# Feed-forward matmuls as pairs on 64 rows that swap PSUM banks halfway, in an attention kernel on one core

## The chip, the core and the metric

The kernel runs on one core of a Trainium2 chip. The core has five engines, each with its own in-order queue of instructions: TensorE (PE) multiplies matrices into PSUM, VectorE (DVE), ScalarE (ACT) and GpSimd (POOL) work element by element, and SyncE (SP) mostly issues transfers between HBM and the on-chip memory. Engines wait for each other through semaphores. PSUM has eight banks of 128 partitions x 512 floats. The metric is the device time of one execution in microseconds (us); smaller is better.

## The reference

With x of 2048 rows and 512 columns, the output is a gated mix of an attention and a feed-forward block:

```python
g = _sigmoid((x * gate_w).sum(-1, keepdims=True))
q = (x @ wq).reshape(B, S, H, Dh)            # 32 heads of 16, S = 2048
k = x @ wk; v = x @ wv                       # one key and value head for all
p = _softmax(einsum("bhqd,bkd->bhqk", q, k) * Dh ** -0.5)
a = (p @ v, heads side by side) @ wo
b = (_gelu(x @ w_gate) * (x @ w_up)) @ w_down     # 512 -> 1376 -> 512
return g * a + (1 - g) * b
```

All data are float32. Each of the 32 heads has 2048 x 2048 scores, and every one of them goes through an exponential.

## The kernel before

The rows of x are cut into four groups of 512 (tg). A prologue projects q, k and v. To keep nearly float32 precision with matmuls that take a rounded operand, each operand is split into a high and a low part (hh and hl, gh and gl, woh and wol), and a product is the sum of three matmuls: high x high, high x low, low x high. The prologue ends with a branch on a flag that all engines read (line 445); its true side is not taken here.

The main loop has 32 units u (a row group, and four heads), each with 16 key chunks kc of 128 keys. A *score step* (`scores`, line 488) fills one of three two-bank PSUM buffers with two matmuls on 51 rows each, one on partitions 0 to 50 and one on 64 to 114, and ACT exponentiates the 128 x 1024 scores into one of twelve buffers p. Two score steps feed one *value step* (`pv`, line 564): four matmuls, each on its own 32 output partitions, that add into the accumulator `acc` in a bank of its own. The chip runs each of these four as two records. After 16 value steps `norm` (line 506) reads the accumulator. For the first unit of a pair it writes two masked copies; for the second it adds to them and queues the division in small parts in the list `bg`, which `slot` hands out one by one after every third feed-forward matmul.

The feed-forward work is the filler between the attention steps. The 1376 hidden columns are cut into 11 chunks of 128, for each of the four row groups: 44 chunks. A chunk's gate output g and up output u take 12 matmuls each (four slices of x, three products); three chunks (at a row group's end two) then give four down outputs of nine (or six) matmuls. When the attention of a row group is done, four outputs of 12 matmuls multiply it by wo. Each output is one call of the generator `units` (line 405): all its matmuls in a row, on 128 rows, into the one bank `pf`, and then a DVE operation that reads it. DVE makes the high parts of the weights (line 105) and POOL the low parts (line 106).

The order is written out by hand: the instructions are recorded as they stand. `ORDER` (line 42) is a unit's pattern, in which S is a score step, V3 three value steps and F one whole feed-forward output:

```python
ORDER = ("V3 SSS F SSS V2 SS V2 SSS F SSS V3 SSS F SSS V3 SSS F SSS V3 SSS F SSS").split()
```

`defer(k, fn)` puts off work by k score steps; `run_later` issues it. SP issues nearly all transfers, in its order: weights (line 205), q (lines 244 and 245), x and wo (line 224), outputs (line 326). PSUM is full: three score buffers of two banks, the accumulator, and `pf`.

Of the kernel before, what the change touches and what calls it, by code (L numbers as in the profile page):

```python
# [19 lines left out]
P = 128  # L20
# [21 lines left out]
ORDER = ("V3 SSS F SSS V2 SS V2 SSS F SSS V3 SSS F SSS V3 SSS F SSS V3 SSS F SSS").split()  # L42
# [3 lines left out]
def mix_kernel(ctx, tc, xT, wq, wkv, wo, wf, out):  # L46
# [3 lines left out]
    ps_s = ctx.enter_context(tc.tile_pool(name="ps_s", bufs=3, space=PSUM))  # L50
    ps_a = ctx.enter_context(tc.tile_pool(name="ps_a", bufs=1, space=PSUM))
    ps_f = ctx.enter_context(tc.tile_pool(name="ps_f", bufs=1, space=PSUM))
    ctx.enter_context(tc.manual_schedule())

# [152 lines left out]
    def split_w(n, lo=None):  # L207
        if n not in stage:
            return
# [5 lines left out]
        lo = lo or nc.gpsimd  # L215
        for t in range(2):
            split(nc.vector, lo, gh[:, t], gl[:, t], st[:, t].rearrange("p (c f) -> p c f", c=NC))
        split(nc.vector, lo, dh, dl, st[:, 2])
        W[n] = gh, gl, dh, dl

    def fetch_split(name, src, hi, lo, h=0):
        cs = slice(2 * h, 2 * h + 2)
        t = cp.tile([P, 2, D], F32, tag="xst", name=f"{name}{h}", bufs=1)
        nc.sync.dma_start(t, src[:, cs])

        def go():
            split(nc.vector, nc.gpsimd, hi[:, cs], lo[:, cs], t)
            if h == 0:
                fetch_split(name, src, hi, lo, 1)

        defer(6, go)

    def reload_x(tg):
        xs[tg] = x_tiles(tg)
        fetch_split(f"xst{tg}_", xT[tg], *xs[tg])
# [3 lines left out]
    def load_qk(t, u):  # L239
        g, ub = divmod(u, 8)  # L240
        b, a = divmod(ub, 2)
        for j in range(2):
            hs = slice(4 * a + j, 4 * a + 4, 2)
            nc.sync.dma_start(t[64 * j : 64 * j + 32].bitcast(F32), scr[g, b, 0:32, hs])
            nc.sync.dma_start(t[64 * j + 32 : 64 * j + KR].bitcast(F32), scr[g, b, 0:16, hs])

    def load_q(u, shift=True, data=True):
        g, ub = divmod(u, 8)
        if data:
            Q[u] = cp.tile([P, 2, TG], F32R, tag="Q", name=f"Q{u}", bufs=2)  # L250
            load_qk(Q[u], u)
        if shift:
            for j in range(2):
                nc.sync.dma_start(Q[u][64 * j + KR : 64 * j + QK].bitcast(F32), shs[g, :, 4 * ub + j : 4 * ub + 4 : 2])
# [3 lines left out]
    for ti, tg in enumerate(order):  # L258
# [4 lines left out]
        for b in range(NB):  # L263
            pq = ps_s.tile([P, 2 * TG], F32, tag="s", name=f"pq{tg}_{b}")[:, 0:TG]
# [5 lines left out]
            if ti == NTG - 1 and b == 0:  # L270
                split_w(0)
            if ti == NTG - 1 and b == 1:
                post_v()
            if ti == NTG - 1 and b == 2:
                load_q(0)
                load_q(1)

    def pairmax():
        pm = ps_s.tile([P, 2 * TG], F32, tag="s", name="pm")[0:1, 0 : 2 * P]
# [12 lines left out]
    peak = []  # L292
    O = {}
    bg = []

    def slot():
        if bg:
            bg.pop(0)()

    def flush():  # L300
        while bg:
            slot()

    wo_jobs = []
    done = [0]

    def pass_list(n):
        return [(i, a, b) for i in range(n) for a, b in ((0, 0), (0, 1), (1, 0))]

    def chain_mm(ps, terms, first=True, last=True):  # L310
        for q, (a, b) in enumerate(terms):
            nc.tensor.matmul(ps, a, b, start=(first and q == 0), stop=(last and q == len(terms) - 1),  # L312
                             skip_group_check=True)
            if q % EVERY == EVERY - 1:
                slot()
            if q == 8 and not peak:
                peak.append(pairmax())
# [10 lines left out]
    def wo_job(g):  # L328
        for i in range(4):
            ps = ps_f.tile([P, D], F32, tag="pf", name=f"wo{g}_{i}")  # L330
            chain_mm(ps, [t for bl in range(NB) for t in wo_terms(g, i, bl)])
            wo_out(g, i, ps)
            yield

    def run_jobs():
        while wo_jobs and wo_jobs[0][0] <= now[0]:
            yield from wo_job(wo_jobs.pop(0)[1])

    def down(batch):
        tg, f = chunks[batch[0][0]]  # L340
        if f == 0:
            acc[tg] = mp.tile([P, 4, D], F32, tag="acc", name=f"acc{tg}", bufs=2)
        for i in range(4):
            ps = ps_f.tile([P, D], F32, tag="pf", name=f"dn{batch[0][0]}_{i}")
            ts = slice(i * P, (i + 1) * P)
            chain_mm(ps, [(a[:, ts], b) for n, hh, hl in batch for dh, dl in (W[n][2:],)
                          for a, b in ((hh, dh), (hh, dl), (hl, dh))])
            o = acc[tg][:, i]
            w = gc[:, 4 * tg + i : 4 * tg + i + 1]
            if f == 0:  # L350
                nc.vector.tensor_scalar(o, ps, w, None, op0=ALU.mult)
            else:
                nc.vector.scalar_tensor_tensor(o, ps, w, o, op0=ALU.mult, op1=ALU.add)  # L353
            yield

    def project(n, t, ps):
        gh, gl = W[n][:2]
        xh, xl = xs[chunks[n][0]]
        chain_mm(ps, [(w[:, t, c], x[:, c]) for c in range(NC) for w, x in ((gh, xh), (gh, xl), (gl, xh))])

    def gate_up(n, hold):
        split_w(n)
        ps = ps_f.tile([P, TG], F32, tag="pf", name=f"g{n}")
        project(n, 0, ps)
        gs = cp.tile([P, TG], F32, tag="gs", name=f"gs{n}", bufs=1)
        sq = cp.tile([P, TG], F32, tag="sq", name=f"sq{n}", bufs=1)
        nc.vector.tensor_copy(gs, ps)  # L367

        def inner():
            nc.vector.scalar_tensor_tensor(sq, gs, GC, gs, op0=ALU.mult, op1=ALU.mult)  # L370
            nc.vector.scalar_tensor_tensor(sq, sq, 1.0, gs, op0=ALU.add, op1=ALU.mult)

        def tanh():
            nc.scalar.activation(sq, sq, AF.Tanh, bias=0.0, scale=GS)  # L374

        def outer():
            nc.vector.scalar_tensor_tensor(sq, sq, 1.0, gs, op0=ALU.add, op1=ALU.mult)  # L377

        chain = [inner, tanh, outer]

        def advance():
            if chain:
                chain.pop(0)()

        for k in (1, 4, 6):
            defer(k, advance)
        yield
        if n == 0:
            ps = ps_a.tile([P, TG], F32, tag="pa", name="u0")
        else:  # L390
            ps = ps_f.tile([P, TG], F32, tag="pf", name=f"u{n}")
        project(n, 1, ps)
        if n == 0:
            yield
        while chain:
            advance()
        hh = cp.tile([P, TG], F32R, tag="hh", name=f"hh{n}", bufs=3)
        hl = cp.tile([P, TG], F32R, tag="hl", name=f"hl{n}", bufs=3)
        nc.vector.scalar_tensor_tensor(gs, ps, 0.5, sq, op0=ALU.mult, op1=ALU.mult)  # L399
        nc.vector.tensor_copy(hh, gs)  # L400
        nc.vector.tensor_sub(hl, gs, hh)
        hold.append((n, hh, hl))
        yield

    def units():
        hold = []
        for n, (tg, f) in enumerate(chunks):
            if n > 0:
                fetch_w(n + 1)
            if n > 0:  # L410
                defer(2 if n == 1 else 8, lambda n=n: split_w(n + 1))
            if n == 2:
                fetch_split("wo", wo, woh, wol)
            yield from gate_up(n, hold)
            if f == NF - 1 and tg + 1 < NTG:
                reload_x(tg + 1)
            if f % 3 == 2 or f == NF - 1:
                yield from down([hold.pop(0) for _ in range(len(hold))])
            yield from run_jobs()

    filler = units()
    nsteps = 8 * NTG * NKC

    def fill(k=1):
        for _ in range(k):
            next(filler, None)
# [7 lines left out]
    fill()  # L434
    fill()
# [3 lines left out]
    split_w(1)  # L439
# [5 lines left out]
    with tc.If(v > 0):  # L445
        with tc.tile_pool(name="gp", bufs=1) as gp:
# [4 lines left out]
            for g in range(NTG):  # L451
                mx = gp.tile([P, 4, H, 2], F32, tag="mx", name=f"mx{g}")
                for ub in range(8):
                    t = gp.tile([P, 2, TG], F32R, tag="gq", name=f"gq{g}_{ub}", bufs=2)
                    load_qk(t, 8 * g + ub)
                    for i in range(4):
                        for h in range(4):
                            rs = slice(64 * (h % 2), 64 * (h % 2) + KR)
                            for e in range(2):
                                ps = ps_s.tile([P, 2 * TG], F32, tag="s", name="gs")  # L460
# [27 lines left out]
    def scores(n):  # L488
        s, pr = divmod(n, 2)
        if s >= nsteps:  # L490
            return
# [5 lines left out]
        ps = ps_s.tile([P, 2 * TG], F32, tag="s", name="s")  # L497
# [8 lines left out]
    def norm(u):  # L506
        g, ub = divmod(u, 8)
        b, a = divmod(ub, 2)
        ac = accp.pop(u)
        if a == 0:  # L510
            flush()
            t = mp.tile([P, TG], F32, tag="nt", name=f"nt{u}", bufs=1)
            tz = mp.tile([P, TG], F32, tag="ntz", name=f"ntz{u}", bufs=1)
# [4 lines left out]
        t, tz = at.pop((g, b))  # L518
        N, z = t, tz
        r = mp.tile([P, TG], F32, tag="nr", name=f"nr{u}", bufs=1)  # L520
# [128 lines left out]
```

## Time and profile before

| | us |
|---|---|
| median of 3 runs | 1304.97 (1304.6 to 1305.59) |
| the profiled execution | 1304.42 |
| its span, first to last instruction | 1302.6 |
| PE busy in it | 1284.3 (99%) |
| ACT busy | 1023.1 (79%) |
| DVE busy | 554.3 (43%) |
| POOL busy | 213.2 (16%) |

Times are counted from the start of the span. In a timeline each row has its start, its length, the engine, the line of the kernel, the operation, the output and its inputs, and how many records were merged; a bracket names idle time ahead of it and what ended it. PE's matmul records overlap, as the next one starts before the last has drained: what one costs is read from start to start. In the rows of groups the first two numbers behind the bar are the busy time in us and the mean of one in ns; the third is the idle time of the engine just before them. PEld is the load of a matmul's weights, which can run under the matmul before. In a table by stretches the columns are the length, and each engine's busy time with its number of records (PE, PEld, DVE, ACT, POOL), then the granted PE clock, the share of the DMA engines and GB/s.

### The profile page before, as it was taken

The page shows a single profiled execution, that of the slowest core. Times are in us where ns is not written, and L with a number is a line of the kernel's source. Part 1 is how long each engine was busy: PE and PEld are TensorE (multiplying, and loading weights), DVE is VectorE, ACT ScalarE, POOL GpSimd, SP SyncE. Part 2 cuts the span into 40 slices and gives each one's busy share as a digit, 9 for nine tenths or more (in the row PEclk, how much of TensorE's full clock was granted, in tenths as well). Part 3 has the DMA queues.
Part 4 walks back from the last instruction along what each step waited for, and adds up shares of the span by engine and source line. Part 5 has one row for each costly group of instructions (what it writes and reads, how often), then busy time and mean ns, then how long its engine had stood idle before and what let it go on. Part 6 is the DMA issues. An engine that isn't in the chain of part 4 may idle for free.

```text
span 1302.6 us, 20297 instructions
## 1 busy us (share of the span) xinstructions
PE 1284.3 (99%) x8180; PEld 647.7 (50%) x8180; DVE 554.3 (43%) x821; ACT 1023.1 (79%) x1118; POOL 213.2 (16%) x172
## 2 busy tenths in 40 slices
PE   9979999999999999999999999999999999999998
PEld 6845445444444444444444554444544454454444
DVE  6763442616352162633426144352526143434344
ACT  5348888888888788888888878878887788888883
POOL 3132121203021021210312011021122011202110
PEclk9989999999999999999999999999999999999999
DMA  8432101111110111111200021110121211001100
GB/s 310 182 102 78 38 15 48 38 62 39 69 38 14 58 61 38 62 37 54 68 19 30 22 86 38 62 38 14 50 70 38 70 38 62 19 20 62 38 1 33
DMA packets 25205, 72.43 MB, mean 56 GB/s; under 512 B 3889, under 2 KB 3921, under 8 KB 25105
## 3 DMA queue, kind: packets, MB, share of 16 engines
q1 hardware_dynamic: 24704, 70.02, 16.0%
q8 instruction: 66, 1.08, 0.3%
q0 software_dynamic: 256, 0.79, 0.1%
q10 hardware_dynamic: 144, 0.26, 0.1%
q14 instruction: 35, 0.28, 0.1%
HBM read 57.67 MB, written 13.37 MB: 55 GB/s over the span
## 4 chain that ended last, share of the span: by engine, by line
PE 82%; DVE 7%; ACT 3%; issue 1%; POOL 0%; DVEq 0%; ACTq 0%
PE acc L570 33%; PE s L500 21%; PE dn L312 9%; PE g L312 8%; PE u L312 8%; ACT p L503 3%; PE wo L312 3%; DVE ntz L536 2%; DVE oh L542 1%; DVE dh L105 1%; DVE nt L539 0%; DVE nr L527 0%; DVE ntz L530 0%; DVE ol L545 0%; DVE nt L533 0%
## 5 line engine op out<-in xcount | busy, mean ns | idle before, releaser
L503 ACT ACTIVATE p<-s 128x1024 f32<-128x1024 f32 x1024 | 972.2, 1027 | 224.9 <-PE s L500 224.5
L570 PE MATMUL acc<-p,v 128*32 128x512 f32 x4096 | 479.2, 597 | 0.0
L500 PE MATMUL s<-Q,kp 51*128 51x512 f32 x2048 | 338.9, 430 | 11.7 <-SPq L445 6.4
L500 PEld LDWEIGHTS s<-Q,kp 51*128 51x128 f32 x2048 | 165.5, 185 | 251.9 <-issue 169.8
L106 POOL TENSOR_TENSOR gl<-st,gh 128x512 fp32r<-128x512 f32 x88 | 122.3, 1409 | 1001.5 <-DVE gh L105 780.9
L570 PEld LDWEIGHTS acc<-p,v 128*32 128x32 f32 x4096 | 113.5, 109 | 259.7 <-issue 252.6
L353 DVE SCALAR_TENSOR_TENSOR acc<-dn,gc,acc 128x512 f32<-128x512 f32 x48 | 35.6, 742 | 206.8 <-PE dn L312 206.8
L367 DVE COPY gs<-g 128x512 f32<-128x512 f32 x44 | 30.4, 691 | 176.3 <-PE g L312 176.2
L312 PE MATMUL dn<-dh,hh 128*128 128x512 f32 x176 | 76.0, 432 | 0.0
L312 PE MATMUL g<-xh,gh 128*128 128x512 f32 x176 | 74.4, 423 | 0.0
L312 PE MATMUL u<-xh,gh 128*128 128x512 f32 x176 | 73.7, 419 | 0.6 <-DVE gs L367 0.6
L312 PE MATMUL g<-xh,gl 128*128 128x512 f32 x176 | 70.0, 398 | 0.3 <-POOL gl L106 0.3
L312 PE MATMUL g<-xl,gh 128*128 128x512 f32 x176 | 69.6, 395 | 0.0
L312 PE MATMUL dn<-dl,hh 128*128 128x512 f32 x176 | 69.0, 392 | 0.0
L312 PE MATMUL u<-xl,gh 128*128 128x512 f32 x176 | 68.8, 391 | 0.0
L312 PE MATMUL dn<-dh,hl 128*128 128x512 f32 x176 | 68.8, 391 | 0.0
L312 PE MATMUL u<-xh,gl 128*128 128x512 f32 x176 | 68.7, 390 | 0.0
L399 DVE SCALAR_TENSOR_TENSOR gs<-u,sq 128x512 f32<-128x512 f32 x44 | 29.9, 679 | 86.5 <-PE u L312 86.3
L105 DVE CAST dh<-st 128x512 fp32r<-128x512 f32 x44 | 64.2, 1459 | 0.0
L106 POOL TENSOR_TENSOR dl<-st,dh 128x512 fp32r<-128x512 f32 x44 | 61.7, 1403 | 0.0
L536 DVE RECIPROCAL ntz<-nr 128x128 f32<-128x128 f32 (+1 forms) x62 | 56.3, 949 | 0.6
L377 DVE SCALAR_TENSOR_TENSOR sq<-sq,gs 128x512 f32<-128x512 f32 x44 | 32.7, 743 | 55.3 <-ACT sq L374 55.3
(113 smaller groups left out, 974.6 us busy)
## 6 DMA issues: line engine op xcount, KB each, us to landing
st<-wf SPq DMA_DIRECT2D x44, 768.0 KB
scr<-q SPq DMA_DIRECT2D x16, 512.0 KB
Q<-scr SPq DMA_DIRECT2D x64, 128.0 KB
Q<-scr SPq DMA_DIRECT2D x64, 64.0 KB
out<-acc SPq DMA_DIRECT2D x16, 256.0 KB
xr<-xT SPq DMA_DIRECT2D x6, 512.0 KB
xst<-xT SPq DMA_DIRECT2D x6, 512.0 KB
xr<-xT SPq DMA_DIRECT2D x4, 256.0 KB
```

Source lines behind the costliest of these rows:

```text
L105: eng_h.tensor_copy(hi, src)
L106: eng_l.tensor_sub(lo, src, hi)
L312: nc.tensor.matmul(ps, a, b, start=(first and q == 0), stop=(last and q == len(terms) - 1), skip_group_check=True)
L353: nc.vector.scalar_tensor_tensor(o, ps, w, o, op0=ALU.mult, op1=ALU.add)
L367: nc.vector.tensor_copy(gs, ps)
L377: nc.vector.scalar_tensor_tensor(sq, sq, 1.0, gs, op0=ALU.add, op1=ALU.mult)
L399: nc.vector.scalar_tensor_tensor(gs, ps, 0.5, sq, op0=ALU.mult, op1=ALU.mult)
L500: nc.tensor.matmul(ps[:, j * TG : (j + 1) * TG], kp[rs, kc * P : (kc + 1) * P], Q[u][rs, pr], start=True, stop=True)
L503: nc.scalar.activation(p, ps, AF.Exp, bias=0.0, scale=SCALE)
L536: nc.vector.reciprocal(z[:, cs], r[:, cs])
L542: nc.vector.tensor_copy(oh[:, cs], N[:, cs])
L570: nc.tensor.matmul(accp[u][32 * j : 32 * j + 32], vt[:, kc], pb[s, j // 2][:, (j % 2) * TG : (j % 2 + 1) * TG], start=(kc == 0), stop=(kc ...
```

## The change

Two feed-forward outputs, z and y, are now computed together as a *job*: gate and up of one chunk, or two of four down outputs, or two of four wo outputs. Every matmul is cut into two of 64 rows. In a first pass over all terms z takes the lower 64 rows of the operands and y the upper 64, pair by pair; in a second pass they swap. Each output adds up in its own bank: y in `pf`, z in one half of the third score buffer, which is lent to the job (the word H) and given back at its end (R). In the meantime score steps use the two other buffers. [...]

Job orders are written out in `WORDS`. In them S is a score step, F3 three pairs and V2 a visit of about two value steps, which is cut where a unit ends or scores are not yet there (`visit` carries the rest over). G and L are gate jobs, D and E the two jobs of a batch of three chunks, d and e those of two, W a wo job, T the rest. The tanh chain of a gate job is put off by 3, 5 and 6 score steps. Splits of weights, x and wo are handed out between pairs like the parts of `norm`; x and wo come in quarters, and weights are fetched two chunks ahead. `norm` now copies the accumulator at once and works from the copy. In the prologue the first two loads of q and the shift rows of kp go through ACT's queue.

```diff
-ORDER = ("V3 SSS F SSS V2 SS V2 SSS F SSS V3 SSS F SSS V3 SSS F SSS V3 SSS F SSS").split()
+WORDS = {
+    "L": "S2 H F3 S F3 S F6 S2 F6 S F6 R S",
+    "G": "V2 S2 V H V F S2 F6 S F3 S F2 S F3 S F3 S F6 R S2 V2 S3 V",
+    "W": "V2 S2 H V2 S F S F6 S F2 S V S F3 S V S F S F S F2 S F3 S V S F6 S R S2",
+    "D": "V H V S2 V2 S2 F6 S F3 S V S F S F5 S F3 S R",
+    "E": "V S3 H V3 S F3 S F6 S2 F6 S F3 R S V2 S3",
+    "d": "V S V H S F3 S F3 S V S F2 S F4 R",
+    "e": "V S V S V S H F3 S F3 S V2 S F5 S F R S",
+    "T": "V2 S3",
+}
...
+    def two_banks(name):
+        i = next(i for i in turn if i not in held)
+        turn.remove(i)
+        turn.append(i)
+        return ps_s.tile([P, 2 * TG], F32, tag=f"s{i}", name=name)
...
+            if ti == NTG - 1 and b >= 2:
+                load_q(b - 2, q=nc.scalar)
...
-            nc.sync.dma_start(kp[r : r + 1].bitcast(F32), row.bitcast(F32))
+            nc.scalar.dma_start(kp[r : r + 1].bitcast(F32), row.bitcast(F32))
...
+    def pair_mm(z, y, X, Y):
+        for half in range(2):
+            for q in range(len(X)):
+                for j, (ps, (a, b)) in enumerate(((z, X[q]), (y, Y[q]))):
+                    lower = (j + half) % 2
+                    rs = slice(64 * lower, 64 * lower + 64)
+                    mm = nc.tensor.matmul(ps, a[rs], b[rs], start=(half == 0 and q == 0),
+                                          stop=(half == 1 and q == len(X) - 1), skip_group_check=True)
+                    if half == 1 and q == 0:
+                        after(mm.ins, relay[0])
...
+                if half == 0 and q == len(X) - 1:
+                    relay = nc.gpsimd.memset(mark, 0.0).ins
+                    for name in behind:
+                        after(relay, name)
+                    relay = [relay.name]
+                if q % EVERY == EVERY - 1 and (half == 0 or q + 4 <= len(X)):
+                    slot(half == 1 or q + 6 <= len(X))
+                yield
...
+    def gate_job(n):
+        tg, f = chunks[n]
+
+        def begin():
+            flush(todo)
+            if n == 1:
+                fetch_w(2)
+            fetch_w(n + 2)
...
+            defer(5 if n == 1 else 2, lambda: todo.extend(split_w(n + 1)))
+            return weights_terms(n, 0), weights_terms(n, 1)
+
+        def end(z, y):
+            gelu(n, z, lambda: y)
+            advance(3)()
+            for k, m in ((3, 2), (5, 1), (6, 0)):
+                defer(k, advance(m))
...
-            nc.vector.tensor_scalar(t, ac, mk, None, op0=ALU.mult)
-            nc.vector.tensor_scalar(tz, ac, mkb, None, op0=ALU.mult)
-            at[g, b] = t, tz
+            nc.vector.tensor_copy(c0, ac)
+            bg.append(lambda: nc.vector.tensor_scalar(t, c0, mk, None, op0=ALU.mult))
+            bg.append(lambda: nc.vector.tensor_scalar(tz, c0, mkb, None, op0=ALU.mult))
+            at[g, b] = c0, t, tz
...
+        c1 = ac
+        if not last:
+            c1 = new("n1")
+            nc.vector.tensor_copy(c1, ac)
...
+    def visit(k):
...
+        want = k + carry[0]
+        left = NKC - at_v[0] % NKC
+        ready = at_s[0] // 2 - at_v[0]
+        take = max(min(want, left, ready, 4), 0)
+        if left - take == 1 and take < 3 and ready > take:
+            take += 1
+        carry[0] = want - take
...
+            elif t[0] == "H":
+                advance(1)()
+                held.add(2)
+                z = ps_s.tile([P, 2 * TG], F32, tag="s2", name="z")[:, 0:TG]
+                y = ps_f.tile([P, TG], F32, tag="pf", name="y")
+                pairs = pair_mm(z, y, X, Y)
+            elif t[0] == "F":
+                for _ in range(k):
+                    next(pairs)
+            else:
+                assert next(pairs, None) is None
+                held.discard(2)
+                turn.remove(2)
+                turn.append(2)
+                job[2](z, y)
```

More of the change, by code (lines that the diff above doesn't have):

```diff
@@ L313, in chain_mm, with after @@
                              skip_group_check=True)
[L314 to L317, printed above, removed]
+    mark = cp.tile([1, 1], F32, name="mark")
+    SYNC = mybir.DependencyInfo(mybir.DependencyClass.Sync, mybir.DependencyReason.DATA)
+    def after(ins, name):
+        tc.add_manual_dep(ins, name, SYNC, reason="a bank passes from one row tile to the other")
+    def pair_mm(z, y, X, Y):
[8 more added lines that the diff above has]
+                        after(mm.ins, relay[0])
+                    if half == 0 and q == 0 and j == 0:
+                        behind = [None, None]
+                    behind[j] = mm.ins.name
+                if half == 0 and q == len(X) - 1:
[6 more added lines that the diff above has]
+                yield
@@ L326, in wo_out @@
         nc.sync.dma_start(out[g * TG + i * P : g * TG + (i + 1) * P], o)
[L328 to L403, printed above, removed]
@@ new lines, in score @@
+    def score():
+        scores(at_s[0])
+        at_s[0] = min(at_s[0] + 1, 2 * nsteps)
+    def visit(k):
+        if at_v[0] == nsteps:
+            return
+        flush(chain if at_v[0] == 0 else [])
+        want = k + carry[0]
[5 more added lines that the diff above has]
+        carry[0] = want - take
+        for _ in range(take):
+            pv(at_v[0])
+            at_v[0] += 1
+        if take and at_v[0] % NKC == 0:
+            if at_v[0] == nsteps:
+                ends.append(None)
+            else:
+                norm(at_v[0] // NKC - 1)
@@ L598, in mix_kernel @@
+    ends = []
+    chain.pop(0)()
+    for k, m in ((2, 2), (4, 0)):
+        defer(k, advance(m))
+    for job in jobs():
+        play(WORDS[job[0]], job)
+    while at_v[0] < nsteps:
+        play(WORDS["T"])
+    flush(chain)
+    flush(todo)
+    now[0] += 16
+    run_later()
+    norm(8 * NTG - 1)
     g = NTG - 1
-    tail = [ps_s.tile([P, 2 * TG], F32, tag="s", name=f"wos{h}")[:, 0:TG] for h in range(3)]
+    tail = [two_banks(f"wos{h}")[:, 0:TG] for h in range(3)]
     tail.append(ps_f.tile([P, TG], F32, tag="pf", name="wof"))
```

259 lines of the change are left out of this document (159 added, 100 removed), and 1 row of the table WORDS.

## The prediction

> **What bounds the kernel now.** I read the page's busy shares first, then its chain that ended last, then who TensorE (PE) waited for.
>
> ```profile
> span 1302.6 us, 20297 instructions
> PE 1284.3 (99%) x8180; PEld 647.7 (50%) x8180; DVE 554.3 (43%) x821; ACT 1023.1 (79%) x1118; POOL 213.2 (16%) x172
> PE 82%; DVE 7%; ACT 3%; issue 1%; POOL 0%; DVEq 0%; ACTq 0%
> L503 ACT ACTIVATE p<-s 128x1024 f32<-128x1024 f32 x1024 | 972.2, 1027 | 224.9 <-PE s L500 224.5
> ```
> ```profile
> PE s L500 <- SPq L445: 6.4, 1, 6.4
> PE s L500 <- ACT p L503: 5.3, 20, 0.3
> ```
> ```profile
> 74.50:1286.00 1211.50, 1205.32 (x7843) 586.11 (x7844) 490.81 (x711) 994.40 (x1068) 193.37 (x134) 1.00 0.14 45
> ```
>
> PE is the bound: 1205.3 of 1211.5 us in the main stage, with only 5.3 us of waits on ScalarE (ACT) there, while ACT idles 224.5 us for PE. So the change is worth what it does to PE's line: the price of its matmuls, of the places where it changes its kind of work, and new waits. A stretch of PE's timeline gives the prices (start, us, and how many records).
>
> ```profile
> 601.98 0.96 PE L500 MATMUL s<-Q,kp 51*128 51x512 f32 x6
> 602.88 0.50 PE L312 MATMUL g<-xh,gh 128*128 128x512 f32 x1
> 603.21 0.40 PE L312 MATMUL g<-xl,gh 128*128 128x512 f32 x1
> 603.45 0.39 PE L312 MATMUL g<-xh,gl 128*128 128x512 f32 x1
> ...
> 605.50 0.39 PE L312 MATMUL g<-xh,gl 128*128 128x512 f32 x1
> 605.82 0.97 PE L500 MATMUL s<-Q,kp 51*128 51x512 f32 x6
> 606.71 2.78 PE L570 MATMUL acc<-p,v 128*32 128x512 f32 x24
> 609.42 0.96 PE L500 MATMUL s<-Q,kp 51*128 51x512 f32 x6
> ...
> 621.86 1.92 PE L570 MATMUL acc<-p,v 128*32 128x512 f32 x16
> 623.71 0.73 PE L500 MATMUL s<-Q,kp 51*128 51x512 f32 x4
> 624.38 1.07 PE L570 MATMUL acc<-p,v 128*32 128x512 f32 x8
> ```
>
> Call a score step S (two 51-row matmuls), a value step V (four matmuls, eight records), a feed-forward matmul F. Three S take 602.88 - 601.98 = 0.90, two take 624.38 - 623.71 = 0.67: one S more costs 0.23, and a block of S costs 0.90 - 3 x 0.23 = 0.21 beyond its steps. Three V take 609.42 - 606.71 = 2.71, two take 1.85: a V costs 0.86, a block 0.13 more. Nine F take 605.50 - 603.45 = 2.05: 0.228 each; the block of twelve takes 605.82 - 602.88 = 2.94, so 0.21 more. The first step of a block shows where the extra goes: its next matmul starts 0.33 later (602.88 to 603.21), 0.10 more than the later ones, because its weights could not be loaded ahead.
>
> **The change, part by part.**
>
> *Blocks.* The F matmuls become pairs on 64 rows, the same form as S, so S and F no longer part into blocks. In the order of the built programs the main loop before has 353 blocks of S, 192 of V, 162 of F: 353 x 0.21 + 192 x 0.13 + 162 x 0.21 = 133 us. After, it has 263 blocks of S with pairs and 263 of V: 263 x 0.34 = 89 us. That is -44 us, and less than 162 vanished F blocks promise, since value visits are cut finer (192 blocks become 263).
>
> *Pairs.* 1704 F become 1704 pairs (two outputs, half the rows, two passes over the terms). The nearest row is S itself, two matmuls on 64-row halves into two banks: 0.23. 1704 x (0.23 - 0.228) = +3. Bounds: 0.2275 (-1) and 0.235 (+12), as blocks of three S cannot show the price in a block of 33. PE issues 1704 more matmuls and loads; the loads hide as those of S do.
>
> *New waits.* I wrote the order of the words out as a walk along PE with these prices, and ACT beside it. The walk needs the delays below.
>
> ```profile
> 602.58 2.86 ACT L503 ACTIVATE p<-s 128x1024 f32<-128x1024 f32 x3 [0.75 <-PE s L500]
> ```
> ```profile
> 605.92 0.69 DVE L367 COPY gs<-g 128x512 f32<-128x512 f32 x1 [6.69 <-PE g L312]
> ...
> 609.56 0.75 DVE L530 SCALAR_TENSOR_TENSOR ntz<-acc,mk,ntz 128x512 f32<-128x512 f32 x1 [1.49 <-PE acc L570]
> ```
> ```profile
> 616.51 0.42 DVE L105 CAST gh<-st 128x512 fp32r<-128x512 f32 x1
> ```
> ```profile
> 617.07 1.35 POOL L106 TENSOR_TENSOR gl<-st,gh 128x512 fp32r<-128x512 f32 x1 [40.95 <-DVE gh L105]
> ```
> ```profile
> 618.47 0.19 PEld L312 LDWEIGHTS g<-xh,gl 128*128 128x128 f32 x1 [0.41 <-POOL gl L106]
> ```
> ```profile
> L106 POOL TENSOR_TENSOR gl<-st,gh 128x512 fp32r<-128x512 f32 x88 | 122.3, 1409 | 1001.5 <-DVE gh L105 780.9 <-issue 207.0 <-PE s L500 13.6
> L105 DVE CAST dh<-st 128x512 fp32r<-128x512 f32 x44 | 64.2, 1459 | 0.0
> L140 POOL MEMSET mk<- 32x1 f32 x4 | 0.4, 92 | 0.1
> ```
>
> An exponential starts 602.58 - 601.98 = 0.60 after the first S of a block (0.50 inside one), takes 1.03, and three take 2.86, so they follow each other at 0.915. PE to VectorE (DVE) takes 0.03 to 0.07 (605.50 + 0.39 to 605.92; 606.71 + 2.78 to 609.56). DVE to GpSimd (POOL) takes 617.07 - 616.93 = 0.14, POOL to PE 618.47 - 618.42 = 0.05. A wait inside a block also exposes one weight load, 0.10.
>
> 1. The relay. After the first pass a one-element memset on POOL must wait for both last matmuls, and the second pass waits for it. No row has PE to POOL; 0.03 (to DVE) and 0.14 (DVE to POOL) bound it and I take the latter, a wait of the same engine. From the start of the last pair: 0.39 + 0.14 + 0.09 (row L140) + 0.05 + 0.10 = 0.77. In the 42 gate jobs (word G) one S stands between, so PE would go on after 0.46: 0.30 each, 42 x 0.30 = +13. In the other jobs V or two S cover it. Queued behind the memset on POOL are the weight splits' subtractions; PE alone waits for it. Bounds: 0.20 each (8 us), or a subtraction of 1.41 ahead of it (a rival).
> 2. The accumulator's one bank. It is now freed by one copy (0.69, row L367) instead of two operations, but V visits follow closer: of 31 changes of accumulator, 17 make V wait: 4 with no score between at 1.3, 7 with two scores at 0.65, 6 with three at 0.4: +12. I allowed 0.3 for DVE being at something else; none gives 7, a 1.46 cast ahead of each (row L105 dh) 32.
> 3. V behind the exponentials. A visit may take the step whose scores were just issued: two S and one V are 0.67 + 0.99 = 1.66, but the second exponential ends 0.60 + 0.915 + 1.03 = 2.55 after the first S began: about 0.9. 17 such places (one of 1.9) and smaller ones: +17.
> 4. S on two buffers. The third is lent to a job from H to R, and 900 of 1024 score steps use the other two. Inside G it fits: nine S against 24 pairs leave 33 x 0.23 = 7.6 us for 9 x 0.915 = 8.2 of ACT, which starts idle. But three S in a row on two buffers (six times, at the end of a W job among others) start the third at 0.56 where its buffer is free at 0.60 + 1.03 + 0.05: 1.14 each; with seven of about 0.4: +10.
> 5. The lent bank itself: in the four e jobs its last score stands directly before the first pair: 4 x 1.27, small ones 3: +8.
> 6. Exposed loads at the waits under 4 and 5 and a few more: +4.
>
> Sum of the waits 13 + 12 + 17 + 10 + 8 + 4 = 64; the 5.3 us on ACT of before go.
>
> *What hides.* 31 copies x 0.69 = 21 us more on DVE, which is 43% busy; the normalization's other steps wait in a list and run between the pairs. 81 memsets x 0.09 on POOL, 16% busy. x and wo come in 128x512 pieces (8 more transfers from SP). The tanh work of a gate job has about 8 us of scores and values before the next pair needs its bank y; it takes five DVE operations and one on ACT,
>
> ```profile
> L374 ACT ACTIVATE sq<-sq 128x512 f32<-128x512 f32 x44 | 28.2, 640 | 1.4 <-DVE sq L371 1.4
> L370 DVE SCALAR_TENSOR_TENSOR sq<-gs 128x512 f32<-128x512 f32 x44 | 30.5, 692 | 3.7 <-DVEq L445 2.3
> ```
>
> 5 x 0.69 + 0.64 = 4.1 us, and waits behind two exponentials. If that cover went, each of 42 jobs would lose what is late.
>
> *The start.* Twelve transfers of Q and two of kp's rows move from SP's queue to ACT's, and the last copy of q stands behind six of them.
>
> ```profile
> 62.23 0.42 SPq L244 DMA_DIRECT2D Q<-scr x1
> ```
> ```profile
> 63.26 0.59 ACT L187 CAST q<-pq 128x512 fp32r<-128x512 f32 x1 [2.86 <-DVE qmx L181]
> ```
>
> Six at about 0.42 to 0.5 make ACT late by up to 3; SP, on which PE waited 6.4 us, is free earlier by as much. I take 0, with 3 either way. SP's fetch of weights now runs two chunks ahead, and waits for the splits of an earlier chunk, as before.
>
> **Sum.** -44 + 3 + 64 - 5 = +18. The profiled execution took 1304.42 us, 1.8 outside its span, 0.55 under the median 1304.97: 1304.42 + 18 = 1322.
>
> **The rivals.**
>
> *Faster: the exponentials keep up.* Items 3 to 5 are 35 us and rest on a walk in which a score buffer comes back 1.7 us after its S. If ACT is ahead at those places, because the earlier waits let it catch up and the visits take older steps, they go with their loads: 1322 - 39 = 1283. For it: ACT idles 224.5 us in all. Against: that idle time came with three buffers, and a wait by PE makes ACT no earlier for a score not yet issued. It decides from 21 us of these 39 on.
>
> *Slower by more: the relay is queued.* POOL takes its work in order, and two subtractions of 1.41 us stand before the relay in a gate job, issued at the third and sixth pair. If DVE gives their casts late, each of 42 relays waits one of them: 42 x 1.41 = 59, for 13: 1322 + 46 = 1368. Against: the sixth pair is 2 us ahead, and DVE is half idle.
>
> *Much slower: loads not hidden.* If a pair's weights could not be loaded under the pair before on the same rows, each pair would cost the 0.33 of a block's first step: 1704 x 0.10 = +170: 1492. Against: the third S of a block follows at 0.23 on the same rows. [...]
>
> *Nothing won:* the blocks' extra stays, if a change between S and pairs costs like one between S and F: 42 to 44 us more, 1366. S, z and y all have 64 x 128 tiles in the built program, so I give it little.
>
> **How the numbers follow.** About 0.2% (2.6 us) is what a measurement of this kernel can tell from no change. Forecast (1308 to 1340) 0.53, relay queued 0.09, the other two slow ones 0.04: slower 0.66. The keeping-up case whole or in great part 0.27: faster. Between them 0.07. Its own range is 1308 to 1340: pairs -4 to +9, relay -5 to 0, accumulator -5 to +6, start 3 either way. For 8 in 10 the range reaches down to 1286, most of the faster case, and up to 1352, a third of the queued relays or DVE late at the accumulator: 1286 to 1352. The signs differ, so the likeliest one's range is the one to read first.
>
> **What would show it.** In PE's timeline z, y and s should follow each other at 0.23 without the 0.33 of a block's first step. PE should wait for POOL's memset some 40 times, about 0.2 each, and for ACT some 60 to 90 times, up to 1.2 each, where it waited 20 times for 0.3 at most; V should wait for DVE's copy at about 17 places. PE's busy share falls to about 95%. Pairs at 0.33, POOL waits of 1.4, or ACT waits under 20 us in sum make the forecast wrong.

## The result, and the profile after

| | before | after |
|---|---|---|
| median, us | 1304.78 (1303.82 to 1305.59) | 1321.64 (1321.19 to 1322.12) |
| the profiled execution | 1304.42 | 1322.12 |
| its span | 1302.6 | 1320.3 |

The changed kernel is slower: 1.013 times the time before, with a 95% interval of 1.0112 to 1.0147. The forecast was 1322.

The page of the changed kernel, with the lines that answer to those shown of before, and the memset that is new:

```profile
span 1320.3 us, 23905 instructions
PE 1286.6 (97%) x9884; PEld 663.8 (50%) x9884; DVE 573.7 (43%) x860; ACT 1034.9 (78%) x1118; POOL 221.4 (17%) x261
PE 88%; ACT 2%; POOL 1%; DVE 1%; issue 1%; DMA 0%; SPq 0%; ACTq 0%; DVEq 0%
L575 ACT ACTIVATE p<-s 128x1024 f32<-128x1024 f32 x1024 | 981.5, 1024 | 226.7 <-PE s L572 219.9
L361 POOL MEMSET mark<- 1x1 f32 x81 | 8.1, 100 | 664.6 <-PE y L353 659.9
```

PE is still the bound. The main stage, from the first score to 16.6 us before the end as in the row shown of before, in the table by stretches:

```profile
74.40:1303.70 1229.30, 1206.45 (x9548) 602.84 (x9548) 511.77 (x753) 1005.83 (x1068) 202.39 (x224) 1.00 0.14 44
```

It is 1229.3 - 1211.5 = 17.8 us longer, which is the whole difference of the spans (17.7), and PE is idle in it for 22.9 us instead of 6.2. So the start of the first score came out at nothing (74.40 for 74.50), and nearly all of the loss stands in PE's idle time. Who ended that idle time, in PE's waits:

```profile
PE s L572 <- ACT p L575: 7.3, 13, 1.0
PE z L353 <- ACT p L575: 5.9, 7, 1.2
PE s L572 <- DVEq L515: 5.7, 1, 5.7
PE acc L645 <- DVE n L586: 4.1, 2, 3.1
PE acc L645 <- DVE n L596: 2.6, 4, 0.8
...
PE z L353 <- POOL mark L361: 0.9, 5, 0.2
```

The 5.7 us behind DVE's queue are the start of the first score (6.4 behind SP's before). Scores and first pairs wait for exponentials (ACT p) 20 times as before, but for up to 1.2 us instead of 0.3, and value visits wait for the copy of the accumulator (DVE n).

These rows hold only the idle time that the modelled ends of matmuls leave visible. A fuller account comes from the starts: each PE instruction's start to the next one's, in groups, less the price of a step and of a block. A stretch of a gate job in PE's timeline shows the prices:

```profile
603.50 0.39 PE L353 MATMUL z<-xh,gh 64*128 64x512 f32 x1
603.50 0.39 PE L353 MATMUL y<-xh,gh 64*128 64x512 f32 x1
603.73 0.40 PE L572 MATMUL s<-Q,kp 51*128 51x512 f32 x2
603.96 0.40 PE L353 MATMUL z<-xl,gh 64*128 64x512 f32 x1
...
605.13 0.39 PE L353 MATMUL z<-xh,gl 64*128 64x512 f32 x1
...
605.36 0.44 PE L572 MATMUL s<-Q,kp 51*128 51x512 f32 x2
605.79 0.50 PE L353 MATMUL z<-xh,gh 64*128 64x512 f32 x1
...
606.13 0.39 PE L353 MATMUL z<-xl,gh 64*128 64x512 f32 x1
```

From a pair to a score and back it is 0.23 each time (603.50, 603.73, 603.96): no block's extra between them. From the last score before the second pass to that pass it is 605.79 - 605.36 = 0.43, so the relay costs 0.20 here; and the second pair of the pass comes 606.13 - 605.79 = 0.34 later, 0.11 more than others. Its weights were not loaded ahead, as the loads of these two pairs show:

```profile
605.79 0.18 PEld L353 LDWEIGHTS z<-xh,gh 64*128 64x128 f32 x1 [0.30 <-POOL mark L361]
...
605.90 0.19 PEld L353 LDWEIGHTS z<-xl,gh 64*128 64x128 f32 x1
```

The relay holds the first load, and the second can only follow it. Summed over the program, from the first score to the last matmul:

| us | before | after | difference | forecast |
|---|---|---|---|---|
| steps (S, V, F or pairs) | 1074.2 | 1078.5 | +4.3 | +3 |
| extra of blocks | 127.6 | 88.1 | -39.5 | -44 |
| waits | 21.7 | 75.0 | +53.3 | +59 |
| sum | 1223.6 | 1241.5 | +17.9 | +18 |

The waits of after are: the relay 9.7 (42 places), a new accumulator 10.1 (13), value visits behind exponentials 13.6 and some 5 more that are booked at the pair behind them, scores 14.8 (24), the first pair of a job 12.6 with those 5, other pairs 9.6, a drop of the clock 2.7, the start 1.7. Those of before are scores 9.6, F 6.3, visits 2.3, the start 3.3. What is called the start here is mostly a half clock behind the first score, which lasts to 77.68 in after and to 80.07 in before.

### The profile page after: what moved, and what is told of

Read it like the earlier page. It is cut to its first block, busy times and chain, and to the rows that moved or that the text cites. A ratio compares the mean times of both kernels' runs of the same rounds, so it can differ in the third digit from the quotient of the medians.

```text
span 1320.3 us, 23905 instructions
## 1 busy us (share of the span) xinstructions
PE 1286.6 (97%) x9884; PEld 663.8 (50%) x9884; DVE 573.7 (43%) x860; ACT 1034.9 (78%) x1118; POOL 221.4 (17%) x261
## 4 chain that ended last, share of the span: by engine, by line
PE 88%; ACT 2%; POOL 1%; DVE 1%; issue 1%; DMA 0%; SPq 0%; ACTq 0%; DVEq 0%
PE acc L645 36%; PE z L353 24%; PE s L572 21%; PE y L353 6%; ACT p L575 2%; POOL gl L123 1%; PE wos L338 1%; DMA Q<-scr 0%; DVE n L596 0%; DVE acc L460 0%; PE wof L338 0%; DVE n L586 0%; POOL mark L361 0%; ACT sq L385 0%; DVE sq L381 0%
## 5 line engine op out<-in xcount | busy, mean ns | idle before, releaser
L353 PE MATMUL z<-xh,gh 64*128 64x512 f32 x344 | 144.1, 419 | 1.2 <-POOL mark L361 0.9
L353 PE MATMUL y<-xh,gh 64*128 64x512 f32 x344 | 144.0, 419 | 0.0
L353 PE MATMUL y<-xl,gh 64*128 64x512 f32 x344 | 135.3, 393 | 0.0
L353 PE MATMUL z<-xl,gh 64*128 64x512 f32 x344 | 135.3, 393 | 0.0
L353 PE MATMUL y<-xh,gl 64*128 64x512 f32 x344 | 133.9, 389 | 0.0
L353 PE MATMUL z<-xh,gl 64*128 64x512 f32 x344 | 133.9, 389 | 0.0
L353 PE MATMUL z<-dh,hh 64*128 64x512 f32 x176 | 70.4, 400 | 5.9 <-ACT p L575 5.9
L353 PE MATMUL y<-dh,hh 64*128 64x512 f32 x176 | 70.6, 401 | 0.0
L353 PE MATMUL y<-dh,hl 64*128 64x512 f32 x176 | 68.9, 391 | 0.0
L353 PE MATMUL z<-dh,hl 64*128 64x512 f32 x176 | 68.8, 391 | 0.0
```

The costliest lines, as they stand in the source:

```text
L353: mm = nc.tensor.matmul(ps, a[rs], b[rs], start=(half == 0 and q == 0), stop=(half == 1 and q == len(X) - 1), skip_group_check=True)
```

## The experiments

The first four ran beside each other (before: 1304.87 there), the next four as well (1304.78), the last by itself (1304.26). The time of after, 1321.64, is that of the result in all of them.

**The relay.** Each output keeps its half of the rows in both passes, and the memset with its waits is gone.

```diff
-                    lower = (j + half) % 2
+                    lower = j
...
-                if half == 0 and q == len(X) - 1:
-                    relay = nc.gpsimd.memset(mark, 0.0).ins
...
```

> The second pass uses the same halves of the rows as the first, so no bank passes from one row tile to the other, and the relay's memset and its waits are gone; the lower half is then counted twice for z and the upper for y, so the output is not the reference's. Everything else stands as in the changed kernel. Theory (the relay costs PE about 0.2 to 0.3 us in each of 42 gate jobs): 1322 - 10 to 13 = 1309 to 1312 us. Rival (the score steps of a job are paced by their exponentials on two buffers, so that what the relay took is waited for one score later): 1319 to 1322 us, with PE's waits for exponentials longer by about as much.

Measured 1309.16 (1308.59 to 1309.81), 12.5 below after. In the account from starts, what stands at the relay's place falls from 9.7 to 2.5, the extra of the pairs behind from 9.6 to 5.2 (42 x 0.11 = 4.6 was to go), and the drop of the clock that is shown below, 2.7 us, is absent. So the relay is on the path: if all 12.5 are its own it costs 0.30 each, and 0.23 if the drop is taken out. Without it the kernel is still 1.0033 times before (1.002 to 1.0045). No run leaves the relay out while the halves still swap.

**Whole rows.** Each pair is one matmul on all 128 rows in this order of jobs; every sum is complete, and no relay is needed.

```diff
-                for j, (ps, (a, b)) in enumerate(((z, X[q]), (y, Y[q]))):
...
+                ps, (a, b) = ((z, X[q]), (y, Y[q]))[half]
+                nc.tensor.matmul(ps, a, b, start=(q == 0), stop=(q == len(X) - 1), skip_group_check=True)
```

> The words, banks and waits of the changed kernel stay, but each pair becomes one matmul on all 128 rows (z in the first pass, y in the second), without a relay; the result is the reference's. Only the form of the feed-forward matmuls differs, so scores and feed-forward part into blocks again: in the program's order 705 blocks of scores, 488 of feed-forward and 263 of values, against 263 of scores with pairs and 263 of values. Theory (a block costs 0.21 us of PE beyond its steps): 930 more blocks x 0.21 = +195, the relay's 10 less, and some 15 us of waits for exponentials that the slower jobs cover: 1322 + 170 = 1492 us, between 1460 and 1510. Rival (changes of form are cheap, and the time lies in the order of the words): under 1400 us.

Measured 1490.41 (1488.37 and 1492.45), as the theory had it. The timeline of this kernel shows what a score between feed-forward matmuls costs when the two do not have the same rows:

```profile
680.94 0.50 PE L559 MATMUL s<-Q,kp 51*128 51x512 f32 x2
681.37 0.50 PE L351 MATMUL y<-xh,gh 128*128 128x512 f32 x1
681.72 0.40 PE L351 MATMUL y<-xl,gh 128*128 128x512 f32 x1
681.96 0.40 PE L351 MATMUL y<-xh,gl 128*128 128x512 f32 x1
682.28 0.50 PE L559 MATMUL s<-Q,kp 51*128 51x512 f32 x2
```

One score and three matmuls take 682.28 - 680.94 = 1.34 where four steps at 0.23 would be 0.92: 0.42 for two changes. The order has 705 blocks of S and 488 of F where the pairs have 263 of S: 930 more. Against the run without a relay that is 1490.41 - 1309.16 = 181 us, or 0.195 each; PE's visible waits from the first score on, the start left out, are nearly the same in the two, 19.9 and 21.1 us. So the 64-row form is what makes it possible to put scores between feed-forward work; it wins only what before did not avoid already with its blocks of three. In the two timelines it is 0.23 between scores and pairs, and some 0.20 more at a change between scores and whole rows; what takes the 0.20 no row shows.

**Half the exponentials,** in after and in before: ACT exponentiates half of each step's scores, and the value steps read that half twice, so that PE's work stays.

```diff
-        nc.scalar.activation(p, ps, AF.Exp, bias=0.0, scale=SCALE)
+        nc.scalar.activation(p[:, 0:TG], ps[:, 0:TG], AF.Exp, bias=0.0, scale=SCALE)
...
```

> Each exponential takes only the first 512 of the 1024 scores of a step, and the value steps use that half twice; the output is not the reference's. PE's work is the same. Theory (some 40 us of PE's waits are for exponentials that come late on two buffers or too close ahead of a value step): an exponential of about half the length takes most of them away, 1322 - 35 = 1287 us, between 1275 and 1297. Rival (these gaps are PE's own, from loads behind semaphores): 1312 to 1322 us.

> The same half exponentials in the kernel before; the output is not the reference's. Theory (before, PE waited only some 5 us for exponentials, since three buffers and whole outputs between the scores gave them time): 1305 - 5 = 1300 us, between 1296 and 1303. If the kernel before falls by 20 us or more, late exponentials are no loss that the change brought.

After falls by 27.2 to 1294.45 (1292.88 to 1294.94), inside the range expected but by less than the 35 of its theory; before falls by 11.7 to 1293.15 (1292.32 to 1293.97), below the range expected, for a theory of 5. Without most waits for exponentials the two kernels are nearly equal. So these waits cost the change 27 - 12 = 15 us and not 27 - 5 = 22: before pays some 12 for them too, where PE's idle time showed 5.3. Most of the difference comes out of the starts, as a place of before shows:

```profile
1276.11 0.73 PE L500 MATMUL s<-Q,kp 51*128 51x512 f32 x4
1277.13 0.50 PE L500 MATMUL s<-Q,kp 51*128 51x512 f32 x2 [0.29 <-ACT p L503]
```

By its prices the third score would start 0.33 + 0.23 = 0.56 after the first, at 1276.67, so it is 0.46 late. The row counts 0.29 of that, as it counts from the modelled end of the score before. Over the 20 places the scores are 8.7 us late instead of the 5.3, and with half the exponentials the time between one score and the next falls by 8.6. The rest is spread over visits and feed-forward steps, and up to 0.8 of it is a shorter half clock behind the start. The loads have a row of their own in the waits of before,

```profile
PEld s L500 <- ACT p L503: 69.2, 134, 0.8
```

but at most of these 134 places the load waits under matmuls that still run, and the score starts no later than its price: with half the exponentials the steps into a block of scores take as long as before.

**The accumulator's copy undone:** the two operations of `norm` read the accumulator itself, as before.

```diff
-            nc.vector.tensor_copy(c0, ac)
-            bg.append(lambda: nc.vector.tensor_scalar(t, c0, mk, None, op0=ALU.mult))
-            bg.append(lambda: nc.vector.tensor_scalar(tz, c0, mkb, None, op0=ALU.mult))
+            nc.vector.tensor_scalar(t, ac, mk, None, op0=ALU.mult)
+            nc.vector.tensor_scalar(tz, ac, mkb, None, op0=ALU.mult)
...
-        if not last:
-            c1 = new("n1")
-            nc.vector.tensor_copy(c1, ac)
...
```

> The kernel after, with one part of the change undone: the two divisor-and-sum operations that read a finished accumulator read it directly again, and the copy that stood ahead of them is gone, so that the accumulator comes free after two vector operations instead of one. Theory: the accumulator copy sits on the path, as the first value visit of the next unit waits for it (13 or 14 waits, 10.1 us in all in the trace of after). One more vector operation of about 0.7 us lies in each of these waits, and some of the changes that were just in time now wait too: 13 to 17 times 0.7, so 9 to 12 us more, 1333 us (1328 to 1340). Rival: the accumulator's change is covered by what stands between two visits, and the copy is a matter of order only: 1319 to 1324.

Measured 1330.25 (1329.78 to 1330.61), 8.6 slower. The waits of visits for DVE in PE's idle time, 6.7 us at 6 places in after, are now

```profile
PE acc L642 <- DVE nt L601: 12.2, 12, 1.6
PE acc L642 <- DVE nz L587: 6.2, 6, 1.6
```

18.4 us at 18 places, 11.7 more. The time rose by less, and one reason can be that the drop of the clock, 2.7 us, is not in this run. The copy at once is worth its place; 8.6 is just under the 9 to 12 of the theory.

**Order in two words.** In W the last three pairs go behind the score that stood after them; in e the lent bank is taken first.

```diff
-    "W": "V2 S2 H V2 S F S F6 S F2 S V S F3 S V S F S V S F2 S F3 S V S F6 S R S2",
+    "W": "V2 S2 H V2 S F S F6 S F2 S V S F3 S V S F S V S F2 S F3 S V S F3 S F3 R S2",
...
-    "e": "V S V S V S H F3 S F3 S V2 S F5 S F R S",
+    "e": "H V S V S V S F3 S F3 S V2 S F5 S F R S",
```

> The kernel after, with only the written order of two job kinds changed: in W the last three pairs of the feed-forward stand after the last but one score, not before it (F6 S R S2 becomes F3 S F3 R S2), and in e the job takes its banks ahead of the first visits (H first, not seventh). Numbers of instructions are the same. Theory: the score buffers are two instead of three while a job holds the lent one, so a score that follows a score too soon waits for an exponential, and the first pair waits for the exponential of the lent buffer; these two waits are 14.8 and 12.6 us in the trace of after, and the two edits take away those of W and e: about 9 us less, 1313 us (1309 to 1316). Rival: the waits are set by the pace of ScalarE as a whole, and move to the next place: 1319 to 1324.

Measured 1311.97 (1311.22 to 1312.32), 9.7 faster. Scores wait 11.0 instead of 14.8 in the account, first pairs 7.3 instead of 12.6, together 9.1 less; these waits did not move elsewhere. The half clock that comes behind the accumulator's longest wait lasts 3.41 us here, 6.83 in after, which can be up to 1.5 us of the 9.7.

**One more step of scores ahead,** on top of these two:

```diff
-    "e": "H V S V S V S F3 S F3 S V2 S F5 S F R S",
+    "e": "H V S V S V S F3 S F3 S V2 S F5 S F R S2",
```

> The kernel of the run with two changed orders, and one more edit: e ends with two scores instead of one, so that from then on one more step of scores stands ahead of the value visits. Theory: the value visits that start a job wait for the exponentials of scores issued shortly before (13.6 us in the trace of after, and some 5 us more that are booked at the pair behind them); with one more step ahead these exponentials are done by then: another 12 us less, 1301 us (1297 to 1306), which is under the 1304.8 of the kernel before. Rival: ScalarE works at 78% over the span and close to all the time in these jobs, so that the visits wait in any case and the scores now wait for the twelve buffers of probabilities: within 3 us of the run with two changed orders.

Measured 1300.04 (1298.94 to 1300.91): 0.9964 times before, 0.995 to 0.9978. Visits behind exponentials fall from 14.7 to 4.4 us, the first pairs from 7.3 to 3.7. The rival holds for a part: scores wait longer for exponentials, 8.2 us instead of 3.4 in PE's idle time. The accumulator's longest wait is 1.9 us instead of 3.1, with no drop of the clock behind it. One S at the end of a word, passed by four e jobs, is worth 12 us in all, and with it the changed kernel beats the one before.

**The copy ahead of the rest.** At a row group's end, the timelines of PE and of DVE in after show why one visit waits longest:

```profile
655.68 3.64 PE L645 MATMUL acc<-p,v 128*32 128x512 f32 x16 [3.11 <-DVE n L586]
```
```profile
651.85 1.51 DVE L617 CAST oh<-nt 128x512 fp32r<-128x512 f32 x1
653.39 1.64 DVE L621 TENSOR_TENSOR ol<-nt,oh 128x512 fp32r<-128x512 f32 x1
654.94 0.68 DVE L586 COPY n<-acc 128x512 f32<-128x512 f32 x1
```

`norm` hands out all that is left in `bg`, and the copy is queued behind it. Before this gap ends the granted clock falls to half (the last but two of the numbers in a row of stretches):

```profile
652.00:654.00 2.00, 0.56 (x4) 0.13 (x4) 1.97 (x2) 1.56 (x2) 2.00 (x2) 1.00 0.79 179
654.00:655.00 1.00, 0.00 (x0) 0.00 (x0) 1.00 (x2) 0.37 (x1) 0.47 (x1) 0.77 0.24 68
655.00:661.00 6.00, 5.32 (x24) 2.05 (x26) 4.45 (x7) 0.43 (x1) 2.79 (x2) 0.50 0.00 0
```

The edit gives the copy a second buffer and issues it first.

```diff
...
-            flush(bg)
-            c0, t, tz = new("n0"), new("nt"), new("nz")
+            c0 = new("n0")
             nc.vector.tensor_copy(c0, ac)
+            flush(bg)
+            t, tz = new("nt"), new("nz")
```

> The kernel after, with the accumulator's copy issued ahead of the vector work that is still outstanding from the row group before (it gets a second buffer for that); all else is the same. Theory: at the changes of a row group this work (oh 1.5 us, ol 1.6 us) stands ahead of the copy in VectorE's queue and TensorE waits 3.1 us for it, after which the granted clock is at half for 6.8 us; both go: 3 us of waits less and 3 of clock, 1316 us (1313 to 1319). Rival: the wait is for the accumulator's last matmul and the clock's drop has nothing to do with it: 1320 to 1323.

Measured 1320.95 (1320.28 to 1321.75): 0.7 below after and inside the rival's range. But the rival's reason does not hold, as wait and drop are gone from the stretch (0.77 and 11.89 busy in after):

```profile
650.00:665.00 15.00, 14.85 (x118) 8.21 (x114) 9.06 (x13) 11.53 (x12) 7.00 (x6) 1.00 0.48 120
```

The account has 3.2 us less at the accumulator and 2.7 less for this drop, and elsewhere 2.6 more at the relay. DVE now reaches the casts of a weight chunk at another time, and POOL has two subtractions ahead of the memset; PE's and POOL's timelines of this kernel:

```profile
810.82 0.44 PE L572 MATMUL s<-Q,kp 51*128 51x512 f32 x2
812.50 0.49 PE L353 MATMUL z<-xh,gh 64*128 64x512 f32 x1 [1.25 <-POOL mark L361]
```
```profile
809.36 2.77 POOL L123 TENSOR_TENSOR gl<-st,gh 128x512 fp32r<-128x512 f32 x2 [13.05 <-issue]
812.08 0.37 POOL L361 MEMSET mark<- 1x1 f32 x1
```

It is the rival of the queued relay, at two places with 1.25 us and one with 0.75. Of the 5.9 us to be won 0.7 came and the relay took 2.6, which leaves 2.6. In the profiled executions 1.6 of these lie in the half clock behind the start: the first score starts at 74.40 in after and at 74.52 in this run, and the half clock lasts to 77.68 and to 80.95, so that PE works in it for 3.28 and for 6.43 us (after, this run, and before):

```profile
70.85:77.68 6.83, 3.28 (x15) 3.14 (x17) 4.49 (x6) 2.20 (x3) 4.00 (x3) 0.50 0.52 165
```
```profile
74.12:80.95 6.83, 6.43 (x30) 6.24 (x32) 5.53 (x9) 4.51 (x5) 1.22 (x1) 0.50 0.58 197
```
```profile
73.25:80.07 6.82, 5.57 (x15) 4.18 (x16) 1.30 (x3) 3.37 (x4) 0.00 (x0) 0.50 0.67 239
```

Whether other executions of the same kernel have it at the same place is not known, as there is one profile of each. About 1 us stays open.

**All together,** with one edit in G besides.

> All edits that lowered the time, together, on the kernel after: the two changed orders, the additional score step at the end of e, the accumulator's copy ahead of the outstanding vector work; and in G the two scores after the first visit are moved ahead of its second value step (V2 S2 V becomes V S2 V2). The run with the last scores took 1300.04 us. Theory: what is left there are waits of their own, so the copy ahead takes the 2.9 us away that the first visit of a row group still waits (it is 1.9 at the longest, and no drop of the clock follows it), and the edit of G some 0.5 us: 1297.5 us (1295 to 1299). Rival: as in the run with the copy ahead alone, the relay gives it back, as its memset then stands behind a subtraction on GpSimd in three or four places (1.25 us at the longest there): 1299 to 1302. Both are under the kernel before, at 1304.8.

Measured 1298.77 (1298.62 to 1300.2), 0.996 times before (0.9947 to 0.9974): the best kernel here, though not told apart from the run with the last scores. PE's idle time:

```profile
PE s L572 <- ACT p L575: 10.0, 31, 0.7
...
PE z L353 <- POOL mark L361: 3.9, 7, 1.2
...
PE acc L646 <- DVE n L597: 0.5, 3, 0.2
PE acc L646 <- DVE n L585: 0.3, 2, 0.2
```

Both expectations hold in part: the accumulator's waits fall from 5.3 to 0.8, and the relay's rise from 1.3 to 3.9, as do the scores' from 8.2 to 10.0.

## Why the prediction was right

The forecast of 1322 hit the time, and its mechanism is the one that the runs show: PE's line, with fewer blocks and more waits. Several terms were off, in both directions, and the sum is closer than its terms deserve.

- *Blocks, -44:* -39.5. The prices of 0.21 and 0.13 were a little high for before (127.6, not 133) and right for after (88.1, not 89). The run on whole rows gave 0.195 a block over 930 blocks.
- *Pairs, +3:* +4.3, at 0.23 as S.
- *"The 5.3 us on ACT of before go":* the step that failed most. Before's waits were 18.4 us without the start, and half the exponentials made before 11.7 faster, so more than 5 were there to go. The term came from one row, that of PE's visible idle time, which leaves out two things: its 20 places cost 8.7 from start to start, and waits of other kinds, 6.3 at feed-forward steps and 2.3 at visits, were not counted as something that goes.
- *The relay, +13:* right in size. 9.7 stand at the second pass's start (0.23 each) and 4.6 at its second pair, and taking the relay out gave 12.5, of which 2.7 can be the clock's.
- *The accumulator, +12:* 10.1 at 13 places, not 17. One of them was 3.1, which the walk along the order did not hold: work left in `bg` stood ahead of the copy. The drop of the clock that it brought, 2.7, was not foreseen at all.
- *V behind the exponentials, +17:* 13.6 and some 5. The run with one more step ahead took 12 of it away.
- *S on two buffers, +10, and the lent bank, +8:* 14.8 and some 8. The two words took 9.7 away.
- *Exposed loads, +4:* 9.6 less the relay's 4.6 is 5.0.
- *The start, 0:* the first score starts 0.1 earlier, but the waits booked behind it are 1.6 less (1.7 for 3.3), 1.1 of them by the shorter half clock. The forecast has nothing that would make it shorter: that is luck.
- *The sums:* the bounds given for the terms add up to -17 and +18, so that the range would begin at 1305, not 1308; three scores on two buffers come to 1.68 - 0.56 = 1.12 each, not 1.14. Neither moves the forecast.

So the waits of after were 73 without the start for 64 (scores 4.8 and the clock 2.7 are most of what is more), those taken off were 18 for 5, and blocks gave 4.5 less: the first makes the sum 9 too low, the second 13 too high, the third 4.5 too low. With the pairs 1.3 too low and the start 1.6 too high, errors of some 15 us stand on each side. That the terms are of the right kind and order is shown; that 1322 came out to a microsecond is luck.

Of the rivals, *the exponentials keep up* (1283) fell: ACT was not ahead at those places, where 41 us of waits stand in the account (13.6, 14.8 and 12.6), and even half the exponentials took only 27 of the 39 away. But part of its condition could be made true by the order: 1300.04 with three edits of words. *The relay is queued* did not occur in after (0.2 at the longest in PE's waits) and did at a few places in the run with the copy ahead. *Loads not hidden* fell on the pairs' 0.23; the time of 1490 in the run on whole rows has another cause, the changes between forms. *Nothing won* fell on the same 0.23. Of what the changed profile was to show, the spacing of 0.23 and the relay's 42 places, 0.2 each, came as told, and so did waits on ACT up to 1.2; but PE's own rows have only 21 waits on ACT and 5 on POOL, the rest being seen in starts alone, and PE is busy 97%, not 95%. In these rows the waits on ACT come to 14.2 us, and under 20 was named as a sign that the forecast is wrong; by the account it is 41, so the sign was tied to a view that does not show these waits in full.

## What to carry to other kernels

Count the changes of form on the bound engine and price them from starts: here each costs 0.2 us, and bringing two kinds of work to one form saved 40 us. Then walk the new order along the buffers that it takes or shares, because the finer mixture gave 53 back, nearly all in waits of 0.2 to 1.2 us; three edits to the written order, found in that walk, took 22 of these away and turned a loss of 1.3% into a gain of 0.4%. Take waits from starts and not from an engine's visible idle time, of the kernel before as well: 20 waits of 5.3 us in its row cost 8.7 from start to start, and the time fell by 11.7 when their cause was halved.

## What the runs showed of the hardware

In after a single gap of 3.11 us on PE came with 6.83 us at a granted clock of 0.50, which cost about as much again as the gap (2.7 us by the account). In the run with two words a gap of 3.11 us came with 3.41 us at 0.50, and in the run without a relay the clock stayed at 1.00 around a gap of 3.10 us.

From 6 to 1320 us of after the granted clock changes at 70.85, 77.68, 654.53 and 661.36. The distances, 6.83, 576.85 and 6.83 us, are 2, 169 and 2 times 3.413. In before it changes at 73.25 and 80.07, again 2 times 3.413 apart. Rows of after, the 3.41 us ahead of 654.53 and the half clock behind it, and then two steps of 3.41 us around the gap of the run without a relay, where 650.11 is about 167 times 3.413 behind the end of the half clock at the start (the mean clock from 75 to 100 is 0.90 there, which puts that end near 80):

```profile
651.12:654.53 3.41, 1.45 (x12) 0.30 (x4) 3.38 (x5) 2.46 (x3) 2.80 (x2) 1.00 0.80 215
654.53:661.36 6.83, 5.68 (x26) 2.31 (x28) 4.92 (x7) 0.79 (x1) 2.79 (x2) 0.50 0.00 2
```
```profile
646.69:650.11 3.42, 2.07 (x20) 0.50 (x12) 3.38 (x6) 2.63 (x4) 2.25 (x2) 1.00 0.15 49
650.11:653.52 3.41, 1.66 (x16) 0.42 (x16) 3.41 (x5) 0.46 (x1) 1.80 (x2) 1.00 0.00 0
```

In after the step ahead of 654.53 holds most of the gap and only 1.45 us of PE's work, and the clock falls at its end, while the gap is still open; in the run with two words it falls behind a step with 0.98. In the run without a relay the gap lies across two steps with 2.07 and 1.66 us of work, and the clock stays. These are three gaps; what decides whether one halves the clock they do not show.
